# Four of seven normalising tiles from VectorE to GpSimd in the head of an attention-and-MLP kernel, q and k turned half a step later, and the first loads reordered

## The chip, the cores and the metric

The kernel runs on one core of one Trainium2 chip. A core has TensorE (PE in the profile, its weight loads PEld), VectorE (DVE), ScalarE (ACT), GpSimd (POOL) and SyncE (SP), which here only issues DMAs. The metric is the device time of one execution in microseconds; a time is the median of several runs.

## What is computed

```python
# q, k, v: (8, 12, 448, 64) float32
scores = scale * np.matmul(q, k.transpose(0, 1, 3, 2))
m = np.max(scores, axis=-1, keepdims=True)
e = np.exp(scores - m)
attn = e / (np.sum(e, axis=-1, keepdims=True) + np.exp(-m) + 1e-09)
x = np.matmul(attn, v)          # then heads side by side: (3584, 768)
h = x @ w_in                    # (768, 2048)
sp = np.where(h > 20.0, h, np.log1p(np.exp(np.minimum(h, 20.0))))
out = (h * np.tanh(sp)) @ w_out # (2048, 768)
```

It is an attention whose softmax has one more term in its denominator, followed by a two-layer network with the mish function between its layers.

## The kernel before

**Tiling.** The 12 heads of a batch entry make 6 pairs, 48 pairs in all; three pairs are a unit. Pairs 0 to 5 (`HEAD = HP`, the first batch entry) are worked off by a loop of their own, `for p in range(HEAD)` at line 511, which I call the head. The loop over units at line 540 does the rest, with the two layers of the network as filler work beside the attention of later batch entries. A pair's 2 x 448 query rows are seven tiles of 128 rows, done in four steps: steps 0 to 2 have two tiles each, step 3 has one.

**One pair.** `load_pair` (L114) issues three DMAs on SP's queue for q, k and v, 224 KB each, into buffers that four pairs share in turn. `cast_pair` (L151) turns them into bf16, all three on POOL (L162, L163, L164), but for pair 0, whose q is cast by DVE and whose k by ACT. `transpose_pair` (L167) turns q and k on PE with eight small transposes (L179) into a PSUM bank that it takes with `mo_take`; there are two such banks. `evac_qk` (L187) copies them to SBUF, in the head on ACT (L198, L218). `scores` (L229) does the matmuls of one step (L255, L258, and L263, L266 for step 3) and the maximum of its rows on DVE (L270); it runs up to three steps ahead, since there are three PSUM buffers for scores. `exps` (L275) takes the exponentials on ACT (L283) with their sums, and frees the buffer. `denominators` (L295) gives `rden`, one over the denominator of each row (L296, L300, DVE).

**Normalising and turning.** `normalise` (L302) multiplies the seven tiles of the buffer `en` by `rden`, in place: in the head on DVE (L317), in a unit for one of its three pairs on POOL (L315, `on_pool`), which then reads a copy of `rden` that DVE makes (L308). Then one DMA (L321, SP's queue) writes the transposed tiles to `eT`. For pairs 5, 6 and 7 (`BY_PE`) there is no such DMA: `turn_on_pe` (L326) transposes them on PE (L332), seven matmuls for each of four column blocks, and DVE copies them out (L336); `TURN_AT` says at which step of a unit. `av_pair` (L344) multiplies `eT` with v (L358). Four buffers `en` are used in turn by pairs (`N_EN`), so the exponentials of pair p overwrite what the transposing DMA of pair p - 4 reads.

**The order of work.** Every engine runs its instructions in the order in which the program issues them. The order is written out by hand: in step s of pair p of the head, the program issues the exponentials of that step, at s = 1 the copies of q and k of pair p + 2, then the scores three steps on, and at s = 0 the loads of pair p + 4, the casts of pair p + 3, one piece of the network's weights (`load_w`, L148, a DMA issued by POOL) and the denominators of pair p - 1. Pair p - 1 is normalised at s = 1. At s = 3 q and k of pair p + 3 are turned, and then pair p - 3 is multiplied with v. SP's queue so takes loads and transposing DMAs in turn, and POOL's takes three casts and one weight piece a pair. Copies out of PSUM by `late` wait until `flush_late` is called in the next step.

**The start.** Lines 499 to 508 load pairs 0, 1 and 2 (q, k, v of each in turn), cast and turn pairs 0 and 1, issue the first three scores, load pair 3 and cast pair 2.

Of the kernel before, what the change touches and what calls it, by code (L numbers as in the profile page):

```python
# [15 lines left out]
UNIT_PAIRS = 3  # L16
# [3 lines left out]
def kernel(  # L20
# [9 lines left out]
    nc = tc.nc  # L30
# [5 lines left out]
    NT = 4  # L36
# [62 lines left out]
    loaded, casted, qkT, att, xT, gT, o_sbs, stats = {}, {}, {}, {}, {}, {}, {}, {}  # L99
# [3 lines left out]
    def flush_late():  # L103
        while late:
            late.popleft()()

    def mo_take():

        if not mo_free:
            flush_late()  # L110
        return mo_free.popleft()


    def load_pair(p):  # L114
        if p >= N_PAIRS:
            return
        b, h0 = p // HP, (p % HP) * 2
        tiles = []
        for nm, src in (("q", q), ("k", k), ("v", v)):
            t = ld_pool.tile([SP_, 2, NT * D], FP32, tag=f"{nm}_f", name=f"{nm}_f")  # L120
            nc.sync.dma_start(
                out=t, in_=src[b, h0 : h0 + 2].rearrange("h (p t) d -> p h (t d)", t=NT)
            )
            tiles.append(t)
        loaded[p] = tiles


    def w_pieces():
# [19 lines left out]
            nc.gpsimd.dma_start(out=dst, in_=src.rearrange("(a p) c -> p a c", p=128))  # L148


    def cast_pair(p):  # L151
        if p >= N_PAIRS:
            return
        q_f, k_f, v_f = loaded.pop(p)
        q_bf = bf_pool.tile([SP_, NT, 2, D], BF16, tag="q_bf", name="q_bf")
        k_bf = bf_pool.tile([SP_, NT, 2, D], BF16, tag="k_bf", name="k_bf")
        v_bf = bf_pool.tile([SP_, 2, NT * D], BF16, tag="v_bf", name="v_bf", bufs=9)
        by_t = "p h (t d) -> p t h d"
        cast_q, cast_k = nc.gpsimd.tensor_copy, nc.gpsimd.tensor_copy
        if p == 0:  # L160
            cast_q, cast_k = nc.vector.tensor_copy, nc.scalar.copy
        cast_q(out=q_bf, in_=q_f.rearrange(by_t, t=NT))  # L162
        cast_k(out=k_bf, in_=k_f.rearrange(by_t, t=NT))  # L163
        nc.gpsimd.tensor_copy(out=v_bf, in_=v_f)  # L164
        casted[p] = (q_bf, k_bf, v_bf)

    def transpose_pair(p, bank=None):  # L167
        if p >= N_PAIRS:
            return
        q_bf, k_bf, _ = casted[p]  # L170
        ps = mo_take() if bank is None else sc_tiles[2][:, bank, :]
        ps_k = sc_tiles[1][:, bank, :] if bank is not None else mo_take() if p == 0 else ps
        by_s = [
            t[:, :].bitcast(BF16).rearrange("p (s n) -> p s n", s=2)[:, s, :]
            for s, t in enumerate((ps, ps_k))
        ]
        for s, src in enumerate((q_bf, k_bf)):
            for t in range(NT):
                nc.tensor.transpose(  # L179
                    by_s[s][:, t * SP_ : (t + 1) * SP_],  # L180
                    src[:, t].rearrange("p h d -> p (h d)"),
                    ident[:SP_, :SP_],
                )
        own = [] if bank is not None else [ps, ps_k] if p == 0 else [ps]
        qkT[p] = (by_s, own)

    def evac_qk(p, act=False):  # L187
        if p >= N_PAIRS:
            return
        (q_ps, k_ps), own = qkT[p]  # L190
        mo_free.extend(own)
        qd = q_diag[p % 3]
        kT = qk_pool.tile([128, S], BF16, tag="kT", name="kT")
        if p < DIAG_FROM:
            qT = qd.rearrange("d i h r -> d (i h r)")[:, 0:S]
            qkT[p] = (qT, kT)
            if act:
                nc.scalar.mul(qT, q_ps[:, 0:S], SCALE)  # L198
            else:
                nc.vector.tensor_scalar(  # L200
                    out=qT, in0=q_ps[:, 0:S], scalar1=SCALE, scalar2=None, op0=ALU.mult
                )
        else:
            qkT[p] = (qd, kT)
            if p < DIAG_FROM + 3:
                nc.vector.memset(qd[0:64, :, 1, :], 0.0)
                nc.vector.memset(qd[64:128, :, 0, :], 0.0)
# [14 lines left out]
    def scores_ahead(limit):  # L222

        while rg["next"] < limit and rg["used"] < len(sc_tiles):
            rg["used"] += 1
            scores(rg["next"])
            rg["next"] += 1
# [67 lines left out]
    def denominators(st):  # L295
        nc.vector.scalar_tensor_tensor(  # L296
            out=st["den"], in0=st["sums"], scalar=1e-9, in1=st["expm"],
            op0=ALU.add, op1=ALU.add,
        )
        nc.vector.reciprocal(out=st["rden"], in_=st["den"])  # L300

    def normalise(p, dma=True, on_pool=False):  # L302
        st = att[p]
        en = st["en"]
        if on_pool:

            st["rden2"] = st_pool.tile([128, NTILE], FP32, tag="rden2", name="rden2")
            nc.vector.tensor_copy(out=st["rden2"], in_=st["rden"])  # L308
        for i in range(NTILE):
            args = dict(  # L310
                out=en[:, :, i, 0:SP_], in0=en[:, :, i, 0:SP_],
                scalar1=st["rden2" if on_pool else "rden"][:, i : i + 1],
            )
            if on_pool:
                nc.gpsimd.tensor_scalar(scalar2=1.0, op0=ALU.mult, op1=ALU.mult, **args)  # L315
            else:
                nc.vector.tensor_scalar(scalar2=None, op0=ALU.mult, **args)  # L317
        eT = eT_pool.tile([128, NT, 2 * S], BF16, tag="eT", name="eT")
        st["eT"] = eT
        if dma:  # L320
            nc.sync.dma_start_transpose(  # L321
                out=eT.rearrange("c j (i q) -> c (j i) q", q=128),
                in_=en.rearrange("q j i c -> q (j i c)"),
            )
# [142 lines left out]
    for g in range(B // 2):  # L467
# [15 lines left out]

    weight = [5.2] + [1.0] * (steps - STEPS) + [0.4] * (STEPS - 1)

    LEAD = UNIT_PAIRS + 1
    LOAD_AT = (0, 3, 6)
    HEAD = HP

    BY_PE = (HEAD - 1, HEAD, HEAD + 1)  # L490
    TURN_AT = (
        {1 + j: [(HEAD - 1, j)] for j in range(NT)},
        {0: [(HEAD, 0), (HEAD, 1)], 1: [(HEAD, 2)], 2: [(HEAD, 3)],
         3: [(HEAD + 1, 0)], 4: [(HEAD + 1, 1)], 5: [(HEAD + 1, 2)], 6: [(HEAD + 1, 3)]},
    )
    AV_AT = ({5: 3, 7: 4, 10: 5}, {5: 6, 8: 7, 10: 8})

    W_AT = ({5: 1, 9: 1}, {1: 1, 4: 1, 5: 1, 7: 1, 9: 1, 11: 1}, {3: 1, 5: 1, 7: 1, 9: 1})
    for p in range(UNIT_PAIRS):
        load_pair(p)  # L500
    for p in range(2):
        cast_pair(p)
        transpose_pair(p)
        if p == 0:
            evac_qk(p, act=True)
            scores_ahead(3)
    load_pair(3)
    cast_pair(2)


    for p in range(HEAD):
        for s in range(STEPS):
            if s == 1 and p == 0:
                transpose_pair(p + 2)
            exps(p * STEPS + s)
            if p == 0 and s == 0:
                evac_qk(1, act=True)
            if s == 1:
                evac_qk(p + 2, act=True)
            if s:  # L520
                flush_late()
            scores_ahead(HEAD * STEPS + 3)
            if s == (2 if p == HEAD - 1 else 0):
                load_pair(p + 4)
            if s == 0:
                cast_pair(p + 3)
                load_w(1)
                if p:
                    denominators(att[p - 1])
            if s == 1:  # L530
                if p:
                    normalise(p - 1)
            if s == 3 and p + 3 < HEAD + 2:
                transpose_pair(p + 3)
            if s == 3 and p >= 3:
                av_pair(p - 3, act=True)
    denominators(att[HEAD - 1])
    normalise(HEAD - 1, dma=HEAD - 1 not in BY_PE)

    for u in range(UNITS_PER_B, N_UNITS + 2 * UNITS_PER_B):  # L540
        attn = u < N_UNITS
# [9 lines left out]
        for n in range(steps):  # L551
            pi, s = divmod(n, STEPS)
            p, idx = p0 + pi, p0 * STEPS + n
# [92 lines left out]
```

## Time and profile before

| what | value |
|---|---|
| median of 3 runs | 490.76 us (488.90 to 491.35) |
| the profiled execution's own time | 492.75 us |
| its span in the profile | 491.0 us |
| granted PE clock, mean | 0.997 |
| PE busy | 450.5 us, 92% of the span |
| DVE busy | 351.3 us, 72% |
| ACT busy | 350.2 us, 71% |
| POOL busy | 161.5 us, 33% |
| DMA | 92.19 MB, mean 188 GB/s |
| L317, normalising on DVE | 238 instructions, 67.2 us, 354 ns each in the mean |
| L315, normalising on POOL | 98 instructions, 61.7 us, 649 ns each in the mean |

The profile is of one execution. Its span runs from the first to the last instruction; the execution's own time is 1.75 us longer. Times in the views count from the start of the span. The page shows the busy time of each engine in 40 slices, the chain of waits follows what released each step back from the end, the timeline lists instructions in order of time and merges neighbours of one kind ("x7"), and the windows sum up the busy time of each engine in a stretch. A square bracket in a timeline row is the idle time of the engine before that row, with what ended it.

### The profile page before, as it was taken

To read this page: it belongs to the slowest core of one execution; us is meant where nothing else is said; L and a number is where in the kernel's file an instruction comes from. 1 tells how busy PE (TensorE), PEld (TensorE's weight loads), DVE (VectorE), ACT (ScalarE), POOL (GpSimd) and SP (SyncE) were. 2 spreads that over 40 slices of the span, in tenths; PEclk is the share of its full clock that TensorE was granted. 3 is DMA by queue.
4 is the path that set the end of the run, shared out by engine and by line. 5 is a ranking of instruction groups with operands and counts; after the bars stand their busy time and mean duration, and the time that the engine had idled before them with its cause. 6 is when DMAs were issued, how large, how long until landed. Compare 5 with 4: busy or idle time off the path is not lost.

```text
span 491.0 us, 8804 instructions
## 1 busy us (share of the span) xinstructions
PE 450.5 (92%) x2992; PEld 248.5 (51%) x2992; DVE 351.3 (72%) x702; ACT 350.2 (71%) x906; POOL 161.5 (33%) x266
## 2 busy tenths in 40 slices
PE   3556898798989999999999999999999999999996
PEld 1222444454644555555655555555556565556563
DVE  4798987978868787878788786878797878420021
ACT  4889678878777887979796878888797979502300
POOL 3622257454412534253413323253425230300000
PEclk9999998999999999999999999999999999999999
DMA  8999999999999999999998979998999686780112
GB/s 212 183 205 228 236 207 221 228 177 236 175 225 263 195 220 188 241 186 267 148 248 187 223 164 210 211 213 227 176 265 179 167 176 140 132 159 21 45 37 93
DMA packets 209452, 92.19 MB, mean 188 GB/s; under 512 B 166272, under 2 KB 205952, under 8 KB 209408
## 3 DMA queue, kind: packets, MB, share of 16 engines
q1 hardware_dynamic: 201920, 85.35, 81.2%
q0 software_dynamic: 7488, 6.29, 8.8%
q8 instruction: 23, 0.38, 0.3%
q14 instruction: 21, 0.17, 0.1%
HBM read 45.61 MB, written 11.01 MB: 115 GB/s over the span
## 4 chain that ended last, share of the span: by engine, by line
PE 68%; DVE 14%; ACT 9%; DMA 4%; issue 2%; SPq 1%; POOL 0%; DVEq 0%; ACTq 0%
PE mo L446 24%; PE mo L382 23%; PE sc L249 8%; ACT en L283 8%; DVE negm L270 7%; PE sc L358 6%; DVE en L317 4%; PE sc L382 3%; PE sc L179 3%; DMA eT<-en 3%; DMA k_f<-in_k_dram 1%; PE mo L358 1%; PE sc L255 1%; DVE xT L367 1%; DVE eT L336 1%
## 5 line engine op out<-in xcount | busy, mean ns | idle before, releaser
L283 ACT ACTIVATE en<-sc,negm 128x448 bf16<-128x448 f32 x336 | 209.7, 637 | 28.7 <-DVE negm L270 16.3
L270 DVE TENSOR_REDUCE negm<-sc 128x2 f32<-128x896 f32 x192 | 182.4, 969 | 61.5 <-PE sc L249 48.7
L446 PE MATMUL mo<-w_out_sb,gT 128*128 128x384 bf16 (+1 forms) x896 | 142.1, 303 | 0.0
L382 PE MATMUL mo<-xT,w_in_sb 128*128 128x448 bf16 x672 | 140.2, 352 | 0.9 <-DVE xT L367 0.9
L388 ACT ACTIVATE gT<-mo 128x448 bf16<-128x448 f32 x112 | 59.4, 543 | 73.5 <-PE mo L382 73.3
L446 PEld LDWEIGHTS <-gT 128*128 128x128 bf16 x896 | 84.0, 98 | 46.8 <-issue 1.3
L382 PEld LDWEIGHTS <-w_in_sb 128*128 128x128 bf16 x768 | 72.8, 98 | 64.9 <-issue 4.2
L315 POOL TENSOR_SCALAR en<-en,rden 128x448 bf16<-128x448 bf16 x98 | 61.7, 649 | 115.8 <-DVE rden L308 106.0
L249 PE MATMUL sc<-kT,qd 128*128 128x448 bf16 x252 | 71.6, 354 | 1.8 <-DVE qd L210 1.5
L162 POOL CAST q_bf<-q_f 112x512 bf16<-112x512 f32 x47 | 29.1, 619 | 121.8 <-DMA q_f<-in_q_dram 105.4
L283 ACT ACTIVATION_READ_ACCUMULATOR en<-sc,negm 128x1 f32 x336 | 69.2, 206 | 0.0
L317 DVE TENSOR_SCALAR en<-en,rden 128x448 bf16<-128x448 bf16 x238 | 67.2, 354 | 0.9
L433 DVE COPY o_sb<-mo 128x384 f32<-128x384 f32 (+1 forms) x64 | 32.1, 502 | 41.3 <-PE mo L446 41.2
L249 PEld LDWEIGHTS <-qd 128*128 128x128 bf16 x252 | 24.0, 97 | 32.1 <-issue 13.9
L358 PE MATMUL sc<-eT,v_bf 112*64 112x448 bf16 x288 | 34.1, 357 | 4.1 <-ACT en L283 2.0
L164 POOL CAST v_bf<-v_f 112x512 bf16<-112x512 f32 x48 | 29.6, 618 | 20.6 <-DMA v_f<-in_v_dram 19.1
L358 PEld LDWEIGHTS <-v_bf 112*64 112x64 bf16 x384 | 21.1, 114 | 25.7 <-issue 16.9
L255 PE MATMUL sc<-kT,qd 64*128 64x448 bf16 x36 | 17.5, 508 | 17.4 <-ACT en L283 16.0
L163 POOL CAST k_bf<-k_f 112x512 bf16<-112x512 f32 x47 | 29.2, 622 | 6.7 <-DMA k_f<-in_k_dram 5.9
L210 DVE TENSOR_SCALAR qd<-sc 64x448 bf16<-64x448 bf16 x72 | 27.8, 386 | 0.9
L218 ACT COPY kT<-sc 128x448 bf16<-128x448 bf16 x39 | 20.8, 534 | 6.8 <-PE sc L179 6.8
L446 PE MATMUL mo<-w_out_sb,mid 128*128 128x384 bf16 x128 | 24.9, 326 | 0.0
(50 smaller groups left out, 306.9 us busy)
## 6 DMA issues: line engine op xcount, KB each, us to landing
q_f<-in_q_dram SPq DMA_DIRECT2D x48, 224.0 KB, 5.5
k_f<-in_k_dram SPq DMA_DIRECT2D x48, 224.0 KB, 5.6
v_f<-in_v_dram SPq DMA_DIRECT2D x48, 224.0 KB, 5.9
w_in_sb<-in_moe_w_in_dram POOLq DMA_DIRECT2D x12, 256.0 KB, 5.6
w_out_sb<-in_moe_w_out_dram POOLq DMA_DIRECT2D x8, 384.0 KB, 8.6
out_dram<-o_sb SPq DMA_DIRECT2D x7, 336.0 KB, 3.5
out_dram<-o_sb SPq DMA_DIRECT2D x8, 288.0 KB, 4.8
out_dram<-o_sb SPq DMA_DIRECT2D x8, 240.0 KB, 3.4
```

Source lines behind the costliest of these rows:

```text
L163: cast_k(out=k_bf, in_=k_f.rearrange(by_t, t=NT))
L164: nc.gpsimd.tensor_copy(out=v_bf, in_=v_f)
L249: nc.tensor.matmul(sc[:, bk, 0:S], lhsT=qT[:, i].rearrange("d h r -> d (h r)"), rhs=kT, start=True, stop=True,)
L270: nc.vector.tensor_reduce(out=negm, in_=sc[:, 0 : len(cols), 0:S], axis=AX.X, op=ALU.max, negate=True)
L283: nc.scalar.activation(out=st["en"][:, :, c, 0:SP_], in_=sc[:, bk, 0:S].rearrange("q (j c) -> q j c", j=NT), func=AF.Exp, bias=st["negm"][ ...
L315: nc.gpsimd.tensor_scalar(scalar2=1.0, op0=ALU.mult, op1=ALU.mult, **args)
L317: nc.vector.tensor_scalar(scalar2=None, op0=ALU.mult, **args)
L358: nc.tensor.matmul(av[h * 64 : (h + 1) * 64, 0:S], lhsT=v_bf[:, h, j * D : (j + 1) * D], rhs=e_h, start=(j == 0), stop=(j == NT - 1),)
L382: nc.tensor.matmul(h_ps[:, 0:S], lhsT=w_in_sb[:, dm, ff * 128 : (ff + 1) * 128], rhs=xT[b][:, dm, :], start=(dm == 0), stop=(dm == DM_T - 1),)
L388: nc.scalar.activation(out=gT[b][:, ff, :], in_=h_ps[:, 0:S], func=AF.Mish)
L433: nc.vector.tensor_copy(out=o_sb[:, cols], in_=st["o"][:, 0:n_cols])
L446: nc.tensor.matmul(st["o"][:, 0:n_cols], lhsT=src[:, ff, c0 : c0 + 128], rhs=w_out_sb[:, ff, cols], start=(ff == 0), stop=(ff == FF_T - 1),)
```

## The change

In the head and for pair 5, `normalise` is called with `shared=4`: tiles 0 to 3 go to POOL and 4 to 6 stay on DVE; POOL reads a copy of `rden`. The call moves from step 1 to step 0 of the pair, ahead of the casts of pair p + 3, so that POOL's order is four tiles, three casts, one weight piece. q and k of pair p + 2 are turned at step 0 of pair p, behind the scores issued there, where they had been turned at step 3 of pair p - 1. At the start, q and k of pairs 0 to 2 are loaded ahead of their v, and cast ahead of them too. PE turns pair 5 one step later in the unit after the head.

```diff
-    def load_pair(p):
+    def load_pair(p, which="qkv"):
...
-        tiles = []
+        tiles = loaded.setdefault(p, [])
         for nm, src in (("q", q), ("k", k), ("v", v)):
+            if nm not in which:
+                continue
...
+    def cast_v(p):
+        nc.gpsimd.tensor_copy(out=casted[p][2], in_=loaded.pop(p)[2])
+
-    def cast_pair(p):
+    def cast_pair(p, with_v=True):
...
         cast_q(out=q_bf, in_=q_f.rearrange(by_t, t=NT))
         cast_k(out=k_bf, in_=k_f.rearrange(by_t, t=NT))
-        nc.gpsimd.tensor_copy(out=v_bf, in_=v_f)
         casted[p] = (q_bf, k_bf, v_bf)
+        if with_v:
+            cast_v(p)
...
-    def normalise(p, dma=True, on_pool=False):
+    def normalise(p, dma=True, on_pool=False, shared=0):
         st = att[p]
         en = st["en"]
-        if on_pool:
+        if on_pool or shared:
 
             st["rden2"] = st_pool.tile([128, NTILE], FP32, tag="rden2", name="rden2")
             nc.vector.tensor_copy(out=st["rden2"], in_=st["rden"])
         for i in range(NTILE):
+            pool_does = on_pool or i < shared
             args = dict(
                 out=en[:, :, i, 0:SP_], in0=en[:, :, i, 0:SP_],
-                scalar1=st["rden2" if on_pool else "rden"][:, i : i + 1],
+                scalar1=st["rden2" if pool_does else "rden"][:, i : i + 1],
             )
-            if on_pool:
+            if pool_does:
                 nc.gpsimd.tensor_scalar(scalar2=1.0, op0=ALU.mult, op1=ALU.mult, **args)
             else:
                 nc.vector.tensor_scalar(scalar2=None, op0=ALU.mult, **args)
...
+    BY_POOL = 4
...
     TURN_AT = (
-        {1 + j: [(HEAD - 1, j)] for j in range(NT)},
+        {2 + j: [(HEAD - 1, j)] for j in range(NT)},
...
-    for p in range(UNIT_PAIRS):
-        load_pair(p)
+    for which in ("qk", "v"):
+        for p in range(UNIT_PAIRS):
+            load_pair(p, which)
     for p in range(2):
-        cast_pair(p)
+        cast_pair(p, with_v=False)
         transpose_pair(p)
...
     load_pair(3)
-    cast_pair(2)
+    cast_pair(2, with_v=False)
+    for p in range(UNIT_PAIRS):
+        cast_v(p)
...
             if s == 0:
+                if p:
+                    denominators(att[p - 1])
+                    normalise(p - 1, shared=BY_POOL)
+                    transpose_pair(p + 2)
                 cast_pair(p + 3)
                 load_w(1)
-                if p:
-                    denominators(att[p - 1])
-            if s == 1:
-                if p:
-                    normalise(p - 1)
-            if s == 3 and p + 3 < HEAD + 2:
-                transpose_pair(p + 3)
             if s == 3 and p >= 3:
                 av_pair(p - 3, act=True)
     denominators(att[HEAD - 1])
-    normalise(HEAD - 1, dma=HEAD - 1 not in BY_PE)
+    normalise(HEAD - 1, dma=HEAD - 1 not in BY_PE, shared=BY_POOL)
```

More of the change, by code (lines that the diff above doesn't have):

```diff
@@ L124, in load_pair @@
             tiles.append(t)
-        loaded[p] = tiles
     def w_pieces():
@@ L148, in load_w @@
             nc.gpsimd.dma_start(out=dst, in_=src.rearrange("(a p) c -> p a c", p=128))
-    def cast_pair(p):
+    def cast_v(p):
+        nc.gpsimd.tensor_copy(out=casted[p][2], in_=loaded.pop(p)[2])
+    def cast_pair(p, with_v=True):
         if p >= N_PAIRS:
             return
-        q_f, k_f, v_f = loaded.pop(p)
+        q_f, k_f = loaded[p][:2]
         q_bf = bf_pool.tile([SP_, NT, 2, D], BF16, tag="q_bf", name="q_bf")
```

## The prediction

> **What bounds the kernel now.** I read the page first: its 40 slices are 12.3 us each, and only the first five (to 61 us) have TensorE (PE) far from full. There DVE and ACT are at 7 to 9 tenths, and the DMA row is full throughout.
>
> ```profile
> PE   3556898798989999999999999999999999999996
> DVE  4798987978868787878788786878797878420021
> ACT  4889678878777887979796878888797979502300
> DMA  8999999999999999999998979998999686780112
> ```
>
> The change touches only this head (pairs 0 to 5 and the first steps of the unit after it). Next the chain of waits from 40 us on, to see what sets the head's end:
>
> ```profile
> 41.25 0.81 POOL q_bf L162
> 42.11 0.55 PE mo L179 x4
> ...
> 49.10 2.00 DVE negm L270 x2
> ...
> 52.44 1.06 DVE en L317 x4
> ```
>
> It goes through a cast of pair 7 that waits for its load, through PE, which turns q and k of pair 7 (L179) ahead of the scores that DVE waits for (1.90 us idle before 45.48), and then through DVE alone. The timeline of DVE shows what L317, the normalising, costs it. Undisturbed, seven tiles take 1.80 us; with three POOL casts beside them 2.98:
>
> ```profile
> 26.80 1.80 DVE L317 TENSOR_SCALAR en<-en,rden 128x448 bf16<-128x448 bf16 x7
> 28.52 2.62 DVE L270 TENSOR_REDUCE negm<-sc 128x2 f32<-128x896 f32 x3
> ...
> 32.71 2.98 DVE L317 TENSOR_SCALAR en<-en,rden 128x448 bf16<-128x448 bf16 x7
> ```
>
> The normalisings of pairs 0 to 4 start at 19.93, 26.80, 32.71, 39.78 and 47.30: 6.84 us a pair. DVE bounds the arithmetic of the head. But behind it stands the SP queue with the DMA. In its timeline one transposing DMA (T0, T1, ... for pairs 0, 1, ...) and one pair's three loads follow each other without a gap from 22.73 to 62.8:
>
> ```profile
> 22.73 5.65 SPq L321 DMA_TRANSPOSE eT<-en  x1
> 28.48 0.53 SPq L121 DMA_DIRECT2D q_f<-in_q_dram  x1
> ...
> 43.50 0.53 SPq L121 DMA_DIRECT2D q_f<-in_q_dram  x1
> ...
> 45.14 12.08 SPq L321 DMA_TRANSPOSE eT<-en  x2
> ```
>
> And the windows of 2 us (PE, PEld, DVE, ACT, POOL busy, clock, then DMA share and GB/s) show the engines' share over 1 nearly everywhere (transfers overlap); it falls to 1 or below in few, these three among them:
>
> ```profile
> 22.00:24.00 2.00, 0.90 (x7) 0.38 (x5) 2.00 (x5) 0.52 (x3) 0.14 (x1) 1.00 0.68 91
> 30.00:32.00 2.00, 0.56 (x2) 0.10 (x2) 1.71 (x5) 2.00 (x7) 0.00 (x0) 1.00 0.82 191
> 46.00:48.00 2.00, 1.21 (x6) 0.37 (x7) 1.97 (x7) 1.97 (x8) 0.00 (x0) 1.00 1.00 178
> ```
>
> So two chains run side by side: DVE's, which the change shortens, and DMA's, whose work it only moves.
>
> **Loads.** All q and k of pairs 0 to 2 before their v. Loads land about 0.97 us apart (casts at 7.67, 8.63, 9.60, 10.57, 11.55, 12.52). k of pair 1 takes the place of q and lands 0.97 us earlier, k of pair 2 two places, 1.95. ACT waited 0.90 us at 9.89 and 0.71 at 12.81 for these transposes; both waits go, and ACT is busy without a break from 12.81 to 22.25. rden of pair 0 (18.67 in the profile) comes 1.6 us earlier, near 17.0. v is needed first at 35.10 (L358), so it costs nothing there.
>
> **Normalising.** Four of seven tiles leave DVE, six times; a copy of rden comes (L308, 0.16 us, some 0.1 of DVE's time). POOL's price is in its own row, seven tiles in 4.33 us, 0.62 each:
>
> ```profile
> 75.34 4.33 POOL L315 TENSOR_SCALAR en<-en,rden 128x448 bf16<-128x448 bf16 x7 [3.50 <-ACT gT L388]
> ```
>
> DVE's three would be 3/7 of 1.72 = 0.74 us alone, but they run beside POOL's four. From the rows above three POOL casts cost DVE 1.18 us, 0.39 each; the first DVE tile runs before POOL starts (0.35 us lie between L308 and L315), so two of them are delayed: 0.74 + 2 x 0.39 = 1.5. The bounds are 0.74 (no delay) and 2.9 (DVE gets in only after all four, 0.25 + 4 x 0.62 + 2 x 0.1). I take 1.5, since the rows show them taking turns. A period without disturbance (26.80 to 32.71: 5.91) becomes 5.91 - 1.72 + 1.5 + 0.1 = 5.8; the two with casts beside them and the one with the 1.90 us hole gain more, because casts now follow the tiles on POOL. ACT needs 7 x 0.615 + 0.10 + 0.85 (q, k) + 0.43 (xT) = 5.65, so it does not stand in the way. rden of pair 5, now 51.35, would be ready near 17.0 + 5 x 5.8 = 46.0.
>
> On this the Trainium skill speaks against the change: "SBUF — State Buffer", section "Who interferes with whom", has VectorE in its two-port modes and GpSimd exclude each other for a whole instruction, the loser blocked. It does not say who comes next; if POOL kept the pair for all four tiles, that would be the 2.9, and the sum rival C's. The rows of 32.71 show turns instead.
>
> **q and k half a step on.** The eight transposes of a pair (1.1 us of PE) are now issued behind the scores of step 0 instead of ahead of them. Nothing is added; the hole at 43.6 to 45.5 shrinks. Their evacuations stay on ACT at step 1, after 1.2 us of exponentials: covered.
>
> **What the DMA makes of it.** T0 needs all seven tiles: 17.0 + 0.35 + 4 x 0.62 + 0.2 (DVE's turns) = 20.0 instead of 22.73, 2.7 us earlier. But POOL's order is now normalising, casts, weight piece. Before, pieces 1 to 3 were issued at 16.00, 18.92 and 21.42, all ahead of T0. Now piece 2 follows the tiles and three casts (20.0 + 1.8, about 21.8) and piece 3 those of pair 1 (about 27). A piece is 256 KB; where nothing else was queued (22 to 24) 91 GB/s moved at a share of 0.68, so it takes 256/(91/0.68) = 1.9 us of the DMA. T0's bytes began some 2 us after its issue with about half of piece 3 to go, so about 1.5 pieces, 2.8 us, move behind T0's start, where pair 8's loads have to wait for them. They also fill the short stretches (30 to 32: 0.18 x 2, and some around 22 and 46), about 0.8 us. Pair 8's load lands 2.7 - 2.8 + 0.8 = **0.7 us earlier**: v (cast at 50.68, so landed about 50.6) at 49.9. The bounds: 2.7 (the pieces cost nothing) and -2.5 (they cost all and T0 gains nothing).
>
> **What is late next.** On POOL the tiles of pair 5 stand behind the casts of pair 8 (L162 to L164) and a weight issue; TensorE's turns of pair 5 (L332) stand behind these tiles, and the later scores of pairs 7 and 8 behind the turns. v at 49.9, cast 0.6, issue 0.72, tiles 4 x 0.62, last transposes 0.4: the first turn ends near 54.1. It ends at 52.09 + 1.82 = 53.9 now, so DVE's lead of 5 us is gone. Left is that one more step of scores (0.5) lies ahead of it, since the turns begin at step 2, and the waits of 0.41 and 0.27 on PE behind it, of which about 0.2 go: 0.7 gained, 0.2 lost. T3 binds at about the same place: pair 7's exponentials overwrite the buffer that it reads, and cannot start before it has landed. From there to the first matmul of the second layer (65.89) PE is nearly full, and everything after it is issued as before, so the rest shifts as a whole.
>
> **The sum:** about 0.5 us off 492.75, the profiled execution's own time: 492.25. That execution stands 2.0 above the median, 490.76; on the median it is **490.3**.
>
> **Rivals**, on the median.
> - A, faster: the DMA is not filled by these pieces, T0's 2.7 us reach pair 8's load, the first turn ends at 52.1, and 2.5 us come off, a little more where PE's waits go too: 488.2. For it: shares over 1 are overlaps, so they do not prove a full DMA. Against it: the loads' issue interval grew from 6.96 (28.48 to 35.44) to 8.06 us (35.44 to 43.50) with a piece beside them.
> - B, slower: POOL's queue. Weight pieces 2 and 3 now stand between T0 and pair 8's load in full, POOL's tiles run at 0.8 instead of 0.62 beside DVE (the longest of L315 is 805 ns), T0 gains only 1.3 us, and pair 5's tiles wait for the late casts. The load comes 1.7 to 2.5 us later than now and the first turn with it, 2.4 to 3.2 us behind the forecast: 493.1. It decides once pair 8's v lands after 50.4, where the loss passes the step won. Against it: the DMA was short of work between 22 and 24.
> - C, the change does not relieve DVE: POOL keeps it out for 2.9 us a pair. A pair takes 7.2, rden of pair 5 comes near 53, its tiles end 0.35 + 4 x 0.62 later and the turn at 56.2, 2.1 us behind the forecast: 492.4. Against it: the turns at 32.71.
>
> **Chances.** Forecast (489 to 491.5) 0.49; A 0.28; C 0.08; B 0.15. Half a per cent, 2.45 us, is about what a measurement of this kernel can tell from no change. Faster by more: nearly all of A, 0.25. Slower by more: that part of B with the load 2 us late or more, 0.12. The rest, 0.63, within. The range takes in A's time and most of B's: 487.7 to 492.9.
>
> **What would show it.** Loads: k of pair 2 cast before 10 us, no wait of ACT until 16. Normalising: three tiles of L317's kind in about 1.5 us, each later one beside a POOL tile, and pairs 5.8 us apart. DMA: T0 issued near 20.0, pair 8's v cast near 50. Tail: PE waits for POOL in front of the first turn of pair 5. I am wrong if the loads of pair 8 land 2 us or more from 49.9, if PE does not wait there, or if a later stage takes the difference back or adds to it.

## The result and the profile after

| what | before | after |
|---|---|---|
| median | 490.02 us (486.46 to 492.13) | 493.12 us (490.96 to 495.92) |
| ratio to before, 95% interval | | 1.0074 [1.0055, 1.0092] |
| profiled execution's own time; span | 492.75 us; 491.0 us | 493.59 us; 491.7 us |
| T1, issue to landing | 9.5 us | 16.8 us |

The change makes the kernel slower by 0.74%; between the medians lie 3.1 us. Intervals come from executions within 1.5% of the fastest of their kernel, which leaves out one each of e10, e16 and e17 below, while medians take in all. The forecast was 490.3, within 487.7 to 492.9, with "no difference" the likeliest. On the page of the changed kernel the difference lies where the change was made, in the fourth slice (36.9 to 49.2 us):

```profile
PE   4463797898989999999999999999999999999996
DVE  4884787997868787978878786878797878420021
ACT  5985776868787797978697978888797979502300
DMA  8899999999999989989898979998999696680112
```

PE has a 3, DVE a 4 and ACT a 5 there, where before had 6, 8 and 9, and the DMA row stays at 9: three engines wait while the DMA engines are busy. The chain of waits of the changed kernel from 25 us on names the wait (start, us, what; rows called issue are left out):

```profile
25.69 0.56 DVE negm L275
26.61 16.82 DMA eT<-en
43.48 1.70 PE mo L364 x8
...
47.53 5.75 DMA k_f<-in_k_dram
...
54.05 0.66 POOL v_bf L153
54.71 0.71 POOL w_in_sb L149
55.46 2.49 POOL en L321 x4
57.99 0.67 PE mo L338 x4
```

One transposing DMA, T1, carries the chain for 16.82 us. Before, no such row stood there: from 25 to 60 us its chain has no DMA, and runs mostly through DVE and PE. SP's timeline gives the issues, first T1 of before and then the changed kernel's:

```profile
30.10 5.25 SPq L321 DMA_TRANSPOSE eT<-en  x1
```

```profile
20.36 4.35 SPq L327 DMA_TRANSPOSE eT<-en  x1
...
26.61 7.70 SPq L327 DMA_TRANSPOSE eT<-en  x1
34.35 0.58 SPq L123 DMA_DIRECT2D q_f<-in_q_dram  x1
...
36.24 10.62 SPq L327 DMA_TRANSPOSE eT<-en  x1
```

T0 is issued 2.37 us earlier than before (22.73) and T1 3.49 earlier (30.10): DVE's side of the change does what it was to do. But T1 lands at 43.4, where before it landed at 39.6 (30.10 + 9.5). Pair 5's exponentials overwrite the buffer `en` that T1 reads, so ACT stops, and PE's product of pair 1 (L364) with it. The rows are from the timelines of ACT (before, then the changed kernel), PE and DVE:

```profile
41.15 0.68 ACT L283 ACTIVATE en<-sc,negm 128x448 bf16<-128x448 f32 x1
```
```profile
43.54 0.63 ACT L288 ACTIVATE en<-sc,negm 128x448 bf16<-128x448 f32 x1 [5.16 <-DMA eT<-en]
```
```profile
43.48 1.70 PE L364 MATMUL mo<-eT,v_bf 112*64 112x448 bf16 x8 [4.75 <-DMA eT<-en]
```
```profile
45.80 0.62 DVE L275 TENSOR_REDUCE negm<-sc 128x1 f32<-128x448 f32 x1 [5.52 <-PE sc L271]
```

Three engines stand still for about 5 us. The first exponentials of pair 4 were 2.36 us ahead of before (31.29 against 33.65); those of pair 5 are 2.39 behind (43.54 against 41.15). The windows of the changed kernel show what the DMA did meanwhile (columns as in the prediction: the last three are PE's granted clock, DMA share, GB/s):

```profile
30.00:32.00 2.00, 1.18 (x6) 0.35 (x7) 1.42 (x2) 2.00 (x9) 2.00 (x4) 1.00 1.24 225
32.00:34.00 2.00, 2.00 (x10) 0.54 (x8) 1.51 (x2) 1.95 (x7) 1.95 (x4) 1.00 1.39 111
34.00:36.00 2.00, 1.35 (x12) 0.82 (x11) 1.74 (x7) 0.97 (x3) 0.49 (x1) 1.00 1.44 118
36.00:38.00 2.00, 0.28 (x2) 0.10 (x2) 1.36 (x2) 2.00 (x6) 2.00 (x4) 1.00 1.34 151
38.00:40.00 2.00, 0.47 (x4) 0.22 (x2) 1.80 (x2) 0.38 (x3) 0.09 (x1) 0.64 1.91 79
```

From 32 us on the share rises and the bytes fall from 225 GB/s to between 79 and 151: packets are under way, and take long. Before, the windows from 32 and 34 moved twice as much at lower shares:

```profile
32.00:34.00 2.00, 0.81 (x4) 0.20 (x3) 2.00 (x5) 2.00 (x8) 1.00 (x2) 1.00 1.18 236
34.00:36.00 2.00, 2.00 (x16) 1.21 (x16) 2.00 (x5) 1.03 (x4) 1.62 (x3) 1.00 1.28 287
```

Who is under way in the changed kernel, by queue from 32 to 38 us (packets, MB, share of 16 engines):

```profile
q1 hardware_dynamic: 1889, 0.48, 99.4%
q0 software_dynamic: 269, 0.26, 38.2%
```

Queue 1 is SP's, here T1; queue 0 is GpSimd's, and 0.26 MB is one weight piece. It is the third, issued 0.84 us behind T1 and landed 11.1 us later, at 38.6. All but 31 of T1's 3584 packets are through by 39 us; it lands 4.4 us after that, with the fourth piece (issued at 33.19) under way.

GpSimd's timeline has the issue of the third:

```profile
27.45 0.76 POOL L149 DMA_DIRECT2D w_in_sb<-in_moe_w_in_dram  x1
...
55.46 2.48 POOL L321 TENSOR_SCALAR en<-en,rden 128x448 bf16<-128x448 bf16 x4
```

The second row is pair 5's four tiles, behind the late casts of pair 8, as the forecast had it. PE's first turn of pair 5 waits for them, and ends at 58.66 instead of 53.91:

```profile
56.16 0.35 PE L338 MATMUL mo<-ident,en 128*112 128x128 bf16 x1 [0.24 <-POOL en L321]
```

The first mish of the network comes 3.74 us late (71.93 against 68.19); of that 2.74 are left at 99 us. Further on the two profiles come closer, to 0.74 us, because the profiled execution of before loses time of its own there (it is 2.7 us over its median); the medians show no such gain.

### The profile page after: what moved, and what is told of

It is laid out like the page before. It is cut to its first block, busy times and chain, and to the rows that moved or that the text cites. A ratio compares the mean times of both kernels' runs of the same rounds, so it can differ in the third digit from the quotient of the medians.

```text
span 491.7 us, 8816 instructions
## 1 busy us (share of the span) xinstructions
PE 447.8 (91%) x2992; PEld 248.4 (51%) x2992; DVE 344.2 (70%) x684; ACT 349.1 (71%) x906; POOL 176.6 (36%) x290
## 4 chain that ended last, share of the span: by engine, by line
PE 72%; ACT 9%; DMA 8%; DVE 7%; POOL 2%; issue 1%; SPq 0%; DVEq 0%; ACTq 0%; POOLq 0%
PE mo L452 25%; PE mo L388 23%; PE sc L254 8%; ACT en L288 7%; PE sc L364 6%; DMA eT<-en 6%; DVE negm L275 3%; PE sc L388 3%; PE sc L184 3%; DMA k_f<-in_k_dram 2%; DVE en L323 2%; PE mo L364 1%; PE mo L338 1%; POOL en L321 1%; PE sc L260 1%
## 5 line engine op out<-in xcount | busy, mean ns | idle before, releaser
L321 POOL TENSOR_SCALAR en<-en,rden 128x448 bf16<-128x448 bf16 x122 | 76.9, 648 | 120.7 <-DVE rden L313 110.0
L323 DVE TENSOR_SCALAR en<-en,rden 128x448 bf16<-128x448 bf16 x214 | 60.2, 353 | 0.9
L364 PE MATMUL sc<-eT,v_bf 112*64 112x448 bf16 x288 | 34.1, 357 | 3.2 <-ACT en L288 1.7
L364 PEld LDWEIGHTS <-v_bf 112*64 112x64 bf16 x384 | 20.7, 113 | 28.7 <-issue 20.0
L153 POOL CAST v_bf<-v_f 112x512 bf16<-112x512 f32 x48 | 29.6, 617 | 11.8 <-DMA v_f<-in_v_dram 10.0
L260 PE MATMUL sc<-kT,qd 64*128 64x448 bf16 x36 | 16.7, 486 | 16.7 <-ACT en L288 15.4
```

The source lines that it names most:

```text
L153: nc.gpsimd.tensor_copy(out=casted[p][2], in_=loaded.pop(p)[2])
L364: nc.tensor.matmul(av[h * 64 : (h + 1) * 64, 0:S], lhsT=v_bf[:, h, j * D : (j + 1) * D], rhs=e_h, start=(j == 0), stop=(j == NT - 1),)
```

## The experiments

The kernels are named by the labels of their runs, and every ratio is to the kernel before, with its 95% interval. Two theories stood at the start. **P**: a weight piece beside T1 stretched it. **Q**: GpSimd's own queue lost the time, pair 5's tiles behind pair 8's casts.

### e1 to e3: the pieces out of the way

e1 is the changed kernel with three pieces at pair 0 and none at pairs 1 and 2:

```diff
-                load_w(1)
+                load_w((3, 0, 0, 1, 1, 1)[p])
```

> The changed kernel, but weight pieces 1 to 3 are issued together behind the casts of pair 3, as early as in the kernel before, none behind those of pairs 4 and 5, then one a pair. Theory P (a weight piece beside the second transposing DMA, T1, is what stretched T1 to 17 us and stopped ScalarE for 5.2 us): T1 lands some 8 us after its issue, ScalarE's stop before pair 5 goes below 1.5 us, pair 8's v is cast near 50 instead of 54.1, and the time falls to between 488 and 490.5. Theory Q (GpSimd's queue alone: the tiles of pair 5 behind the casts of pair 8, whose load would be late anyway): v of pair 8 is cast after 53 again, and the time stays at 492 to 494.

Measured: 488.12 us, ratio 0.9961 [0.9942, 0.9980]. T1 lands 8.7 us after its issue, v of pair 8 is cast at 49.41, pair 5 starts 2.73 us ahead of before and the first mish 1.92 ahead. The same change, with two DMA issues moved, is faster than before instead of slower: P, in its broad form.

e2 is the changed kernel, and e3 the kernel before, without the head's six pieces. Both leave work out: half of `w_in` is filled with zeros instead of loaded, and beside that memset DVE's first cast takes 2.78 us in e2 and 2.95 in e3, where it took 0.43.

```diff
+    for _ in range(6):
+        pieces.popleft()
+    nc.gpsimd.memset(w_in_sb[:, :, 0 : d_ff // 2], 0.0)
...
                 cast_pair(p + 3)
-                load_w(1)
```

> The changed kernel without the six weight pieces of the head; the half of w_in that they would fill is set to zero instead, so part of the weights is left out. Theory P: with no piece in the way the lead of 2.4 us that the changed kernel has at pair 4 is kept or grows: pair 8's v is cast before 49, and the time is 486 to 488.5. Theory Q: the tiles of pair 5 still wait behind the casts of pair 8; at best 490.

> The kernel before with the same six pieces left out and the same half of w_in zeroed: the control of the run without pieces. Theory P: the pieces cost the kernel before little, since three of them ran ahead of the first transposing DMA: 488.5 to 490.5, and the changed kernel without pieces is faster than this one by 1 to 3 us. If this one gains as much as the changed one does, the pieces are a load on both and do not explain the difference.

Measured: e2 487.86 us, 0.9950 [0.9928, 0.9971]; e3 488.73 us, 0.9973 [0.9952, 0.9994]. T1 lands after 7.0 and 8.8 us. Without pieces the changed kernel is not slower than the old one. The two intervals overlap, so this pair does not show that it is faster.

### e4 and e10: parts of the change alone

e4 is the kernel before with the loads of the change and nothing else (`load_pair`, `cast_v` and `cast_pair` as in the change):

```diff
-    for p in range(UNIT_PAIRS):
-        load_pair(p)
+    for which in ("qk", "v"):
+        for p in range(UNIT_PAIRS):
+            load_pair(p, which)
...
+    for p in range(UNIT_PAIRS):
+        cast_v(p)
```

> The kernel before with one part of the change: q and k of pairs 0 to 2 loaded and cast ahead of v. All theories: no wait of ScalarE until 16 us and the denominators of pair 0 some 1.6 us earlier. Whether that reaches the end: by the DMA account of the prediction (work only moved) at most 0.5 us, 489.5 to 490.3; if the head's arithmetic sets the end, 1.6 us, 488.4.

Measured: 489.77 us, 0.9994 [0.9971, 1.0017]. The lead of 1.78 us at pair 1 is 0.10 at pair 6: pair 7's cast waits 7.25 us for its load and takes it back.

e10 is the kernel before with q and k turned at step 0:

```diff
+                if p:
+                    transpose_pair(p + 2)
...
-            if s == 3 and p + 3 < HEAD + 2:
-                transpose_pair(p + 3)
```

> The kernel before with q and k transposed at step 0, half a step earlier, and nothing else. Forecast by the steps: it costs nothing and shrinks the hole of DVE near 44; DMA and the weight pieces stay as before, so the time stays within 1 us of the kernel before (ratio 0.998 to 1.002). If the transposes stood in the way of the scores, the ratio would be over 1.002.

Measured: 489.67 us, 1.0003 [0.9977, 1.0030]. Neither part alone gains or costs anything that shows; what the change does, for good or ill, comes with the shared normalising and GpSimd's new order, or with the parts together.

### e5: the changed kernel once more

> The changed kernel as it is, for a second profile. If the stretch of T1 to 17 us belongs to the order of the pieces, it is seen again (T1 lands over 12 us after its issue) and ScalarE stops for more than 3 us before pair 5. If it was a chance of one execution, T1 lands 8 to 9 us after its issue.

Measured: 493.3 us, 1.0042 [1.0005, 1.0079]. T1 lands after 17.2 us and ACT stops for 5.56 us on it. The stretch is no accident of one execution.

### e6 and e7: the third piece, and the fourth

In e6 two pieces are issued at pair 0, the next at pair 1 (22.0, 4.6 us ahead of T1), and none beside T1. In e7 the third stays beside T1, none is issued at pair 3 and two at pair 5. From the changed kernel, the one and the other:

```diff
-                load_w(1)
+                load_w((2, 1, 0, 1, 1, 1)[p])
```
```diff
-                load_w(1)
+                load_w((1, 1, 1, 0, 1, 2)[p])
```

> The changed kernel with one weight piece alone moved: the third, issued beside T1, goes out together with the first behind the casts of pair 3; the second stays where it is. Theory P, in its narrow form (the piece beside T1 does it): T1 lands some 8 us after its issue, the stop of ScalarE goes, 488 to 490. If the fourth piece, issued 5.7 us later, does it as well, T1 is still slow and the time stays above 491.

> The changed kernel with the fourth piece moved back to go out with the sixth, the third left beside T1. Theory P, narrow: T1 is still slowed by the third (lands more than 10 us after its issue), but the empty stretch of the DMA from 39 to 41.5 us goes if it came from the fourth; 490.5 to 492.5, between e1 and the changed kernel. If only the fourth did the harm: 488 to 490.

Measured: e6 487.58 us, 0.9960 [0.9936, 0.9984]; e7 492.58 us, 1.0050 [1.0024, 1.0076]. Moving one DMA of 256 KB turns a loss of 0.7% (0.4% in e5, measured beside e6) into a gain of 0.4%. In e6 the windows from 32 and 34 us move more than twice the bytes of the changed kernel's:

```profile
32.00:34.00 2.00, 2.00 (x10) 0.58 (x10) 1.55 (x2) 1.99 (x7) 1.99 (x4) 1.00 1.28 290
34.00:36.00 2.00, 1.47 (x12) 0.82 (x11) 1.70 (x7) 0.92 (x3) 0.45 (x1) 1.00 0.93 237
```

In e7 the third piece alone stretches T1 to 16.0 us and stops ACT for 4.34; what the fourth adds is the rest, about a microsecond.

### e8, e11 and e12: is there a second cause, and what is the sharing worth?

e8 is e1, and e12 is e6, with pair 5's seven tiles on DVE, so that GpSimd's queue no longer stands ahead of PE's turns:

```diff
-    normalise(HEAD - 1, dma=HEAD - 1 not in BY_PE, shared=BY_POOL)
+    normalise(HEAD - 1, dma=HEAD - 1 not in BY_PE)
```

e11 is e1 with all tiles of the head on DVE:

```diff
-    BY_POOL = 4
+    BY_POOL = 0
```

> The kernel of e1 with the seven tiles of pair 5 on VectorE again, so that TensorE's turns of pair 5 no longer stand behind the casts of pair 8. Theory Q as a second cause (the queue on GpSimd still costs something once the pieces are out of the way): the first turn starts before 50 us instead of 51, and 0.5 to 1.5 us come off e1: 486.6 to 487.7. If the landing of T3, which the exponentials of pair 7 wait for, binds at the same place, nothing changes: 487.6 to 488.6.

> The changed kernel with three weight pieces issued at pair 0 (as in the first experiment, 0.9961 of before) and all seven tiles of the first six pairs on DVE again; the loads and the half step stay. If the sharing with GpSimd is worth what the forecast's rows gave (DVE's seven tiles 1.80 us against 1.12 measured for three, and T0 2 us earlier), this one is slower than the first experiment by 0.5 to 2 us: ratio 0.997 to 1.000. If the gain of the first experiment is that of the pieces' place alone, the ratio is 0.995 to 0.997, the same as with the sharing.

> The changed kernel with the third piece issued at pair 0 (487.58, 0.996 of before) and pair 5's seven tiles on DVE (0.9946 with three pieces first): both mends together. P: the two add little to each other, ratio 0.993 to 0.996, T1 under 6.5 us as SP's row, the first turn of pair 5 near 51. If GpSimd's queue at pair 5 mattered as much as the piece (Q), it would be 0.992 or less.

Measured: e8 487.77 us, 0.9946 [0.9920, 0.9972]; e11 489.43 us, 1.0001 [0.9980, 1.0023]; e12 487.85 us, 0.9976 [0.9950, 1.0002]. In e8 the first turn no longer waits (51.00, all seven at once; in e1 51.51, tile by tile), but its ratio is not told apart from e1's, and e12's is above e6's with intervals that overlap: Q is at most a small second cause. e11 is slower than e1 (their intervals touch at 0.9980) and than e8, which differs from it in the sharing of pairs 0 to 4 alone (their intervals do not overlap): the sharing is what gains, some 0.4 to 0.6%. The first two normalisings in e11's DVE timeline show where that comes from; seven tiles beside POOL's casts take 3.55 us, where e1 has three in 1.29, and T0 leaves at 21.35 instead of 20.43:

```profile
17.77 3.55 DVE L323 TENSOR_SCALAR en<-en,rden 128x448 bf16<-128x448 bf16 x7
...
25.40 1.81 DVE L323 TENSOR_SCALAR en<-en,rden 128x448 bf16<-128x448 bf16 x7
```

### e9: the piece beside T1 in the kernel before

The old kernel's third piece is held back until T1's input is ready, by a copy on GpSimd that reads one element of it:

```diff
-                load_w(1)
+                load_w((1, 1, 0, 1, 1, 1)[p])
...
                     normalise(p - 1)
+                if p == 2:
+                    mark = st_pool.tile([128, 1], BF16, tag="mark", name="mark")
+                    nc.gpsimd.tensor_copy(out=mark, in_=att[1]["en"][:, 0, NTILE - 1, 0:1])
+                    load_w(1)
```

> The kernel before, with one thing moved: its third weight piece (GpSimd issues it at 21.42 there, ahead of T0) is held back by a copy of one element of pair 1's normalised scores, so that it is issued when T1 is, near 30.3, and nothing else of the change is made. P (a piece issued beside T1 stretches it, whatever the kernel): T1, which took 5.25 us as SP's row and landed about 8 us after its issue, takes 7.5 us or more as SP's row and lands 12 us or more after its issue; the exponentials of pair 5 stop on it, and the time is 1 to 3 us over the kernel before (ratio 1.002 to 1.006). Rival R (the stretch needs what the change brings with it, such as T1's earlier place among the loads): SP's row of T1 stays under 6 us and the ratio is 0.997 to 1.001, since a piece ahead of T0 is gone.

Measured: 489.26 us, 1.0008 [0.9981, 1.0035]. (T1 of the kernel before lands after 9.5 us, not the 8 that the expectation names.) T1's row on SP is 6.86 us, between the two expectations; it lands after 11.8, and ACT does not stop. P falls in its simple form. The piece was issued at 27.45, T1 at 27.51, and from 30 to 32 us queue 0 moved 0.20 MB, nearly the whole piece: it went ahead of T1's bytes. "Beside" was too coarse; the order matters.

### e13 to e15: ahead or behind, one piece or two

Theory S: a piece issued behind a transposing DMA moves among its bytes. Theory W: it takes two pieces waiting in the software queue. e13 is e9 with eight copies instead of one, so that the piece comes behind T1:

```diff
+                    for i in range(8):
-                    nc.gpsimd.tensor_copy(out=mark, in_=att[1]["en"][:, 0, NTILE - 1, 0:1])
+                        nc.gpsimd.tensor_copy(out=mark, in_=att[1]["en"][:, 0, NTILE - 1, 0:1])
```

e14 is the changed kernel with its third piece ahead of pair 5's casts (e15 does the same for every pair, without the conditions):

```diff
+                if p == 2:
+                    load_w(1)
                 cast_pair(p + 3)
-                load_w(1)
+                if p != 2:
+                    load_w(1)
```

> The kernel before with its third weight piece held back as in e9, but by eight one-element copies on GpSimd instead of one, so that it is issued about a microsecond behind T1 and not just ahead of it. Theory S (a piece issued behind a transposing DMA moves among its bytes and stretches it; one issued ahead moves first): T1's row on SP is 7 us or more, T1 lands 12 us or more after its issue, the exponentials of pair 5 stop on it for 1 us or more, and the time is 1 us or more over e9's (ratio 1.003 to 1.007). Theory W (the stretch needs two pieces waiting in the software queue): one piece only, so T1 stays as in e9 (row near 6.9) and the ratio is 0.998 to 1.002.

> The changed kernel with one pair of lines exchanged at pair 2: the third weight piece is issued behind pair 1's four tiles and ahead of pair 5's casts, near 25.9 and so ahead of T1 (near 26.6), instead of behind the casts at 27.45. Nothing else changes, and two pieces (the second of 21.96, the third) still stand in the queue at once. Theory S: the piece moves ahead of T1's bytes, T1's row is 5 to 7 us, no stop of 5 us on ACT, and the ratio to before is 0.994 to 0.999. Theory W: T1 is stretched as before, row 7.5 or more, the stop stays, and the ratio is 1.003 to 1.008.

> The changed kernel with each of the six weight pieces of the head issued ahead of that pair's casts instead of behind them, right behind the four tiles, and so just ahead of the transposing DMA that these tiles release. Theory S: no transposing DMA has a piece among its bytes, rows of T1 and T2 5 to 7 us, ratio 0.993 to 0.998, at least as good as e14. Theory W: pieces 2 and 3 still overlap in the queue, T1's row 7.5 or more, ratio 1.002 or more.

Measured: e13 490.32 us, 1.0008 [0.9984, 1.0032], piece 1.68 us behind T1, T1 lands after 14.3 and stops ACT for 2.57. e14 488.93 us, 0.9982 [0.9962, 1.0003], piece 0.80 ahead, T1 lands after 12.9 (its SP row is 7.70, no shorter than in the changed kernel) and stops ACT for 1.48. e15 494.2 us, 1.0082 [1.0046, 1.0118].

Both theories lose something. W is wrong for e14, which has two pieces and no loss (and for e16 and e17 below, which lose with one). S has e13's stop but not its time, and its mechanism is not what e13 shows: by its queues from 32 to 36 us no packet of the piece moved at all, and yet T1 moved 0.59 MB in 4 us, 148 GB/s at a share of 1.28, where that queue of before moved 1.04 MB at 1.22, loads among it:

```profile
q1 hardware_dynamic: 2313, 0.59, 128.2%
```

e15 shows the same trouble one place on. T1 is well (10.7 us), but the piece of pair 5 is now issued at 45.18, 1.20 us behind T3 (43.98); T3 lands after 13.5 us and pair 7's exponentials stop for 4.10 us on it. Putting every piece ahead of the casts mends nothing in general: each piece has to be placed against the DMAs.

### e16 to e18: does the distance decide?

Up to here a piece 0.84 to 1.20 us behind moved among the transposing DMA's bytes, and one 1.59 us or more behind waited until its bytes were nearly through. Theory D took that distance for the rule; rival V said that the stretch was something else of the changed kernel. e16 and e17 are e13 with `range(4)` and `range(5)`; e18 is the changed kernel with six such copies ahead of its third piece:

```diff
                 cast_pair(p + 3)
+                if p == 2:
+                    mark = st_pool.tile([128, 1], BF16, tag="mark", name="mark")
+                    for i in range(6):
+                        nc.gpsimd.tensor_copy(out=mark, in_=att[1]["en"][:, 0, 0, 0:1])
                 load_w(1)
```

> The kernel before with its third piece held back by four one-element copies: by the rows of e13 (0.23 us a copy) it is issued about 0.74 us behind T1. Theory D (the distance decides: 0.6 to 1.2 us behind means among T1's bytes): T1's row on SP is 7.5 us or more, ACT stops 3 us or more on it at pair 5, ratio 1.002 to 1.007. Rival V (the stretch is something else of the changed kernel): T1's row is 6 to 7 us as in e9 and e13, the stop under 3 us, ratio 0.998 to 1.002.

> The same with five copies: the piece is issued about 0.98 us behind T1. Theory D: as with four, T1's row 7.5 us or more and a stop of 3 us or more, ratio 1.002 to 1.007. Rival V: row 6 to 7 us, stop under 3 us, ratio 0.998 to 1.002.

> The changed kernel with six one-element copies on GpSimd ahead of its third piece, so that it is issued about 28.9 and 2.2 us behind T1 instead of 0.84, and nothing else. Theory D: the piece waits until T1 has ended, T1's row is 5 to 7 us, the stop of ACT at pair 5 is under 3 us, and the ratio falls from 1.0042 to 1.0092 to 1.002 or less. Rival V: T1's row stays at 7.5 or more, the stop at 4 us or more, ratio 1.003 to 1.008.

Measured: e16 495.75 us, 1.0136 [1.0095, 1.0178]; e17 491.93 us, 1.0057 [1.0023, 1.0090]; e18 492.57 us, 1.0045 [1.0023, 1.0068]. V falls with e16 and e17: the kernel before, with one piece 0.66 or 0.91 us behind T1 and nothing else of the change, is slower than before, and ACT stops on T1 in both. This is e16's row in the view of DMA issues, microseconds from issue to landing last, and in ACT's timeline:

```profile
eT<-en SPq DMA_TRANSPOSE x1, 13.5
```
```profile
42.16 0.63 ACT L283 ACTIVATE en<-sc,negm 128x448 bf16<-128x448 f32 x1 [2.31 <-DMA eT<-en]
```

D falls too. T1's row on SP stays under 6 us in e16 and e17, so that row is no measure of the stretch; and e18's piece, 2.22 us behind, did not wait for T1's bytes but moved beside them, and the loss stayed. In e18 the two windows from 34 us look like those of the changed kernel:

```profile
34.00:36.00 2.00, 1.32 (x10) 0.72 (x11) 1.85 (x7) 1.07 (x3) 1.08 (x2) 1.00 1.41 100
36.00:38.00 2.00, 0.38 (x2) 0.11 (x2) 1.25 (x2) 2.00 (x7) 1.98 (x4) 1.00 1.55 61
```

### All kernels side by side

The third piece's issue against T1's (minus: ahead), T1 from issue to landing, and ACT's stop at the start of pair 5 that ends with T1:

| kernel | piece to T1, us | T1 lands after, us | stop, us | ratio |
|---|---|---|---|---|
| e2, e3 (no pieces) | none | 7.0, 8.8 | 0, 0 | 0.9950, 0.9973 |
| e1, e8, e11 | over 10 ahead | 8.7, 9.1, 9.4 | 0, 0, 0 | 0.9961, 0.9946, 1.0001 |
| e6, e12 | -4.6 | 9.8, 9.6 | 0, 0 | 0.9960, 0.9976 |
| before, e4 | -8.7 | 9.5, 10.3 | 0, 0 | 1, 0.9994 |
| e15 | -1.94 | 10.7 | 0 (4.10 at T3) | 1.0082 |
| e14 | -0.80 | 12.9 | 1.48 | 0.9982 |
| e9 | -0.06 | 11.8 | 0 | 1.0008 |
| e16 | +0.66 | 13.5 | 2.31 | 1.0136 |
| after, e5 | +0.84 | 16.8, 17.2 | 5.16, 5.56 | 1.0074, 1.0042 |
| e7 | +0.87 | 16.0 | 4.34 | 1.0050 |
| e17 | +0.91 | 14.2 | 2.93 | 1.0057 |
| e13 | +1.68 | 14.3 | 2.57 | 1.0008 |
| e18 | +2.22 | 14.8 | 3.06 | 1.0045 |

Shown, in both kernels: with the piece issued behind T1, T1 lands after 13.5 to 17.2 us and ACT stops for 2.3 to 5.6 us; with the piece ahead or away, T1 lands after 7.0 to 12.9 and ACT stops for 1.5 or not at all. In the times, six of the seven measurements with the piece behind are slower than before by their intervals (e13 is not), and none of the others but e15, whose piece is behind T3.

The same shows at a DMA that no edit was aimed at. T5, the transposing DMA of pair 8, has two pieces 0.4 and 1.1 us behind it in the profiles of e12 and e15, and lands after 17.1 and 14.1 us; with its pieces ahead it lands after 7.0 to 9.8 in the other profiles of the table. The row is e12's:

```profile
eT<-en SPq DMA_TRANSPOSE x1, 17.1
```

But standing behind is neither always that dear nor the only thing that slows a transposing DMA. T0 of the changed kernel has the second piece 1.60 us behind it and lands after 9.2 us (7.7 in e1, which has none there); T4 in e7 has one 0.34 us behind and lands after 8.9; T2 in e8, with its piece 0.81 ahead, lands after 11.8. What sets T1 apart from T0 was not tested; the loads of pair 6 are issued just before T1 (24.77 to 25.96), while all loads issued before T0 had landed by 19.3.

Open: why a piece behind slows a transposing DMA even while the piece itself does not move (e13); what sets the stretch between 13.5 and 17.2, and why T0 and T4 escape it; why e13's time does not show its stop; and e16's 6 us, since its profiled execution was its fastest (490.77, the others 495.3 to 500.5), so that the profile does not show what the other five lost.

## Why the prediction was wrong

**Right: loads.** k of pair 2 was cast at 9.28 (forecast: before 10), ACT did not wait between 9 and 16, and rden of pair 0 came at 16.93 (near 17.0).

**Right: normalising, and cheaper than forecast.** These are the first three normalisings on DVE of the changed kernel, and POOL's row for the second:

```profile
17.24 0.82 DVE L323 TENSOR_SCALAR en<-en,rden 128x448 bf16<-128x448 bf16 x3
...
22.98 1.12 DVE L323 TENSOR_SCALAR en<-en,rden 128x448 bf16<-128x448 bf16 x3
...
28.72 1.12 DVE L323 TENSOR_SCALAR en<-en,rden 128x448 bf16<-128x448 bf16 x3
```
```profile
23.26 2.57 POOL L321 TENSOR_SCALAR en<-en,rden 128x448 bf16<-128x448 bf16 x4 [0.55 <-DVE rden L313]
```

Three tiles took 0.82, 1.12, 1.12 and 1.13 us in pairs 0 to 3 where I took 1.5 (1.30 and 1.54 in pairs 4 and 5, behind the stop); pairs followed each other at 5.74 us (16.74, 22.48, 28.22) where I took 5.8; T0 was issued at 20.36 (20.0). Rival C, with 2.9 us, is out. The Trainium skill ("SBUF — State Buffer", "Who interferes with whom") has VectorE in its two-port modes and GpSimd shut each other out for a whole instruction. The trace shows a wait for one tile of each, and not for a whole instruction of the other: in pair 1 DVE's third took 0.63 us instead of 0.33 and POOL's first 0.72 instead of 0.63; in pair 0 DVE lost nothing and POOL's first took 0.95. I had two DVE tiles delayed by 0.39 each; two were done or under way when POOL came, and one was delayed, by 0.30. What four POOL tiles do beside a longer run of DVE tiles is not shown.

**Right, as far as it shows: q and k half a step on** (e10: 1.0003 [0.9977, 1.0030]).

**Wrong: "What the DMA makes of it".** The failing step is its price: "it takes 256/(91/0.68) = 1.9 us of the DMA", and "about 1.5 pieces, 2.8 us, move behind T0's start, where pair 8's loads have to wait for them". It let a piece take its own bytes' time from whatever comes next, wherever it stood. I had the third piece's issue right (about 27, measured 27.45) and the T1 that it would stand behind, and did not look at the pair. T1 took 16.8 us to land, against 9.8 with one piece moved (e6) and 8.7 with two (e1): 7 us for one piece, not 1.9. And what waited for it was not pair 8's loads first, but T1's own landing and with it pair 5's exponentials. v of pair 8 was cast at 54.05 instead of landing at 49.9. With the piece moved, it is cast at 49.41 (e1) and 48.53 (e6).

**Wrong: what is late next.** The coupling by the four `en` buffers was in my text, but only for T3 and pair 7 ("T3 binds at about the same place"). It bound at T1 and pair 5, one round earlier, for 5.16 us; T1 had 1.5 us of slack there before (landed 39.6, pair 5 at 41.15). The change by itself did not use it up: in e6, without a piece beside T1, it landed at 36.4 and pair 5 began at 38.29. The stretch did. The tail that I did work out, GpSimd's tiles behind the late casts, came as foreseen (PE waits of 0.24 to 0.26 us for each) and no gain from taking it away is told apart from nothing (e8 against e1).

**The sum.** With the third piece moved alone, the kernel measures 487.58 (e6), 0.4% under before: the -0.5 us of my sum was too small as well, and rival A's 488.2 was the better account of everything but that piece. About 2.4 us of gain (490.02 to 487.58) and 5.5 us of loss (487.58 to 493.12) make the result. Two slips change nothing: ACT's terms add up to 5.69, not 5.65, and the matmul at 65.89 (L382, with `w_in`) belongs to the first layer of the network, not to the second.

**Rival B** gave 493.1 and the place, weight pieces 2 and 3 and a late load of pair 8, and its condition (v after 50.4) was met. That its time is the measured one is luck, since its mechanism was not what happened: it priced the pieces at 1.9 us each, put POOL's tiles at 0.8 us (measured 0.64) and T0's gain at 1.3 us (measured 2.37), and had no stop at pair 5.

## What to carry to other kernels

When an edit moves instructions within an engine's queue, the DMAs among them move too: write down the new issue time of each beside those of the large transfers of the other queues, and treat a small transfer that now lies behind a transposing one as a risk of several microseconds, not as its own bytes. Then follow every buffer that the stretched transfer reads to its next writer; with four buffers in turn, 1.5 us of slack was all there was before. A row of microseconds from issue to landing shows such a stretch at once, and SP's own row does not (e16: 4.97 us on SP, 13.5 to landing).

## What the hardware showed that I had not expected

- **A piece of 256 KB issued 0.7 to 2.2 us behind T1 slows it**: 13.5 to 17.2 us to landing against 7.0 to 12.9, in both kernels. Its packets are not more but slower. In the changed kernel those of queue 1 took 51 ns in the mean from 32 to 38 us (99.4% of 16 engines over 1889 packets), in e6 18 ns from 32 to 34 us, and there the queue was alone:

```profile
q1 hardware_dynamic: 2269, 0.58, 127.6%
```

- **The piece may stand still meanwhile.** In the changed kernel the second piece, issued at 21.96, moved nothing between 22 and 26 us: the view by queue has a single row there, T0's.

```profile
q1 hardware_dynamic: 3011, 0.77, 112.0%
```

  The Trainium skill ("DMA: Bandwidth & Descriptors", "Queues, rings and completion order") says that a DMA engine goes round the queues that have work, a packet at a time. The third piece beside T1 agrees with that (99.4% and 38.2% from 32 to 38 us); the second piece here and the third in e13 do not show it, unless their descriptors were not there yet, which no run shows.
- **PE's clock** stands at 0.50 in the changed kernel's records from about 40 to 64 us, behind the stop of three engines, and at 1.00 before that. A score matmul of L260 took 0.53 us in that stretch (at 54.13) and 0.53 at 6.23, but 0.35 at 37.72; the record is 1.00 at both of the last two, so the record alone does not tell this matmul's time, and no price of the 0.50 is seen.
